# Transposing q and k of two pairs of heads by DMA, and placing the last batch's loads one by one, in a fused attention and mixing kernel

## The chip, the cores and the metric

One NeuronCore of a Trainium2 chip runs the kernel. The metric is the device time of one execution in microseconds (us). A time is 1.7 to 2.5 us longer than the span that the profile shows, which runs from the first to the last instruction. "At 88" means 88 us from the start of the span.

## The reference

Four batches, eight heads, 768 positions of 64 values. Causal attention within a window of 128 positions, with the first four positions always visible ("sinks"); its output is `x`, which a mixing layer takes:

```python
keep = is_sink | in_window
a = softmax(where(keep, q @ k.T / sqrt(64), -1e9))
x = a @ v                                   # heads side by side: 768 x 512 per batch
theta = x @ w_theta
zr, zi = x * cos(theta), x * sin(theta)
y = w_tok_r @ zr + w_tok_i @ zi             # along the sequence
u = x + y
out = u + maximum(u @ w_ch, 0)
```

## The kernel before

Heads go two by two, so there are 16 pairs: 8 to 11 are the third batch, 12 to 15 the last. A "slot" is the work on one pair, with a piece of the batch before's mixing woven in. The order on TensorE, ScalarE, GpSimd and SyncE is that of the program text; VectorE's order is made by a scheduler when the kernel is built. GpSimd casts q, k and v to bf16 ahead of their use. Tiles that the profile names: `sc` the scores, `E` their exponentials (ScalarE), `tp` a transpose of q or k by TensorE, `avp` the product with v, `x_nat` is x, `cs` cos and sin of theta (ScalarE; this part at the end of a batch's attention is the "phase stage"), `zz` holds zr and zi, `yp` sums y, `u` and `uT` are u and its transpose, `of` is the output.

q and k are needed with the 64 values of a head on the partitions, for two heads at once. TensorE transposes them into PSUM and ScalarE copies them out in another order of the columns; only the last batch's are transposed by DMA, straight into their final place, which asks for loads in rows of 256 bytes:

```python
QK_DMA = range(12, NPAIR)                   # pairs transposed by DMA, loaded in 256 byte rows
...
def transposed_by_dma(i):
    if i not in QK_DMA:
        return
    for name in ("q", "k"):
        c = qk_c.pop((name, i))             # bf16, cast by GpSimd
        x = qkt.tile([P, S], BF16, name=f"{name}T", tag=f"{name}T")
        nc.sync.dma_start_transpose(out=x.rearrange("c (t p) -> c t p", t=NT),
                                    in_=c.rearrange("p t h d -> p (t h d)"))
        qk_t[name, i] = x

def transposed(name, i):
    if i in QK_DMA:
        return
    c = qk_c.pop((name, i))
    tp = ps_sm.tile([P, NT, P], BF16, name="tp", tag="sm")
    for t in range(NT):
        nc.tensor.transpose(out=tp[:, t, :], in_=c[:, t, :, :], identity=ident)
    x = qkt.tile([P, S], BF16, name=f"{name}T", tag=f"{name}T")
    dst, src = x.rearrange("c (p t) -> c p t", t=NT), tp.rearrange("c t p -> c p t")
    ...
    nc.scalar.copy(out=dst, in_=src)        # VectorE for three early pairs
```

On the same SyncE queue are all loads but eight small ones of sink values, all stores of `of`, and two other transposes: `uT` (ahead of the product with `w_ch`, tile `wp`) and `xT` (ahead of `theta`, tile `thp`).

The values of the sinks of the third and last batch are put in place by VectorE, four instructions a batch, at the start of the third batch:

```python
def sink_values(b):
    for tb in range(NB):
        nc.vector.tensor_scalar(out=vsinks[b % 2][:, tb, :, 0:D], in0=vsf[:, b - 2, :, :],
                                scalar1=rows[:, tb:tb + 1], scalar2=None, op0=ALU.mult)
...
            if b > 1:
                slot(i, (p, hp))
                if b == 2 and hp < 2:
                    sink_values(2 + hp)
            else:
                ...
                if hp == 1:
                    load_later_sinks()      # loads vsf
...
        if b < 3:                           # at the end of the batch's attention
            for n in range(2):
                load_qk(HP * 3 + 2 * (b - 1) + n)
                load_v(HP * 3 + 2 * (b - 1) + n)
        thetas(b, 0)
```

The softmax here doesn't subtract the row's maximum and nothing guards it: scores larger than these inputs give would overflow.

## Time and profile before

| | before |
|---|---|
| median of 4 executions (range), us | 187.97 (187.84 to 188.6) |
| span in the profile, us | 186.9 |
| TensorE busy | 171.9 us, 92% |
| copy of q or k from PSUM on ScalarE, median | 0.80 us |

The part of the profile that counts here is the list of TensorE's waits: what it waited for, us in total, times, and the longest. The second line shown is the passage into the third batch, the first in part (0.6 of its 1.4 us) the passage into the last.

```profile
PE yp L350 <- DVE zz L321: 1.4, 3, 0.6
...
PE wp L378 <- DVE uT L371: 0.9, 1, 0.9
```

### The profile page before, as it was taken

Reading aid. Unit: us, or ns where it says so; the run is one execution under the profiler, and the core shown is the slowest. Engines: PE = TensorE matmul, PEld = TensorE weight load, DVE = VectorE, ACT = ScalarE, POOL = GpSimd, SP = SyncE. Lnnn points to the kernel's source line nnn. Section 1 sums busy time; section 2 is a strip of 40 time slices with the busy share of each in tenths; the row PEclk is TensorE's granted clock in tenths of the full one; section 3 lists DMA queues with packets and bytes.
Section 4 is the critical chain, followed back from the end, with each engine's and each line's share of the span. In section 5 each row is a group of like instructions: output and inputs, shape, how many; then the busy total and the mean of one; then the engine's idle time right before and its main releaser. Section 6 shows DMA issues by size and latency. Waiting matters only on the chain.

```text
span 186.9 us, 4095 instructions
## 1 busy us (share of the span) xinstructions
PE 171.9 (92%) x1655; PEld 88.8 (48%) x1655; DVE 125.7 (67%) x235; ACT 101.5 (54%) x109; POOL 68.7 (37%) x87
## 2 busy tenths in 40 slices
PE   6597998999998998997999999989999999999991
PEld 2344573544464655443455555423445554444550
DVE  6486776782967788189978683797786834824451
ACT  4876778617973661899855801797545019300000
POOL 8965468967886601314545001660000000000000
PEclk9999999999999999999999999999999999999997
DMA  5999999999999995990229769994654311034413
GB/s 183 310 299 205 308 394 345 369 354 334 355 360 340 283 245 154 282 207 4 68 65 165 168 100 271 282 194 59 150 119 100 98 60 56 0 87 109 141 59 114
DMA packets 68275, 36.42 MB, mean 195 GB/s; under 512 B 56352, under 2 KB 62752, under 8 KB 68256
## 3 DMA queue, kind: packets, MB, share of 16 engines
q1 hardware_dynamic: 66960, 35.99, 70.2%
q0 software_dynamic: 1152, 0.04, 0.5%
q8 instruction: 13, 0.21, 0.5%
q10 hardware_dynamic: 144, 0.13, 0.2%
q14 instruction: 6, 0.05, 0.1%
HBM read 25.82 MB, written 6.29 MB: 172 GB/s over the span
## 4 chain that ended last, share of the span: by engine, by line
PE 58%; DVE 14%; ACT 14%; DMA 6%; issue 3%; SPq 2%; POOL 0%; DVEq 0%; ACTq 0%
PE yp L350 22%; PE wp L378 9%; PE thp L308 8%; DMA vf<-in_v_dram 6%; PE avp L255 5%; PE sc L209 5%; DVE zz L321 4%; ACT E L222 4%; ACT cs L317 3%; ACT cs L318 3%; SPq L116 2%; PE tp L183 2%; DVE E L225 2%; PE xtp L285 2%; DVE vsink L467 2%
## 5 line engine op out<-in xcount | busy, mean ns | idle before, releaser
L222 ACT ACTIVATE E<-sc 128x1024 bf16<-128x1024 f32 x48 | 48.4, 1027 | 23.4 <-PE sc L209 17.5
L350 PE MATMUL yp<-zz,wrT 128*128 128x512 bf16 x138 | 52.4, 379 | 1.6 <-DVE zz L321 1.4
L350 PE MATMUL yp<-zz,wiT 128*128 128x512 bf16 x138 | 52.5, 380 | 0.4 <-ACT wiT L337 0.3
L225 DVE TENSOR_TENSOR E<-E,mask 128x768 bf16<-128x768 bf16 (+1 forms) x27 | 26.2, 981 | 13.2 <-ACT E L222 13.1
L75 POOL TENSOR_SCALAR q<-qf 128x768 bf16<-128x768 f32 x14 | 13.4, 958 | 44.2 <-PE tp L183 23.3
L321 DVE TENSOR_TENSOR zz<-cs,x_nat 128x1024 bf16<-128x1024 bf16 x24 | 20.2, 878 | 10.3 <-ACT cs L318 10.3
L378 PE MATMUL wp<-wch,uT 128*128 128x512 bf16 x92 | 23.6, 379 | 1.0 <-DVE uT L371 0.9
L381 DVE SCALAR_TENSOR_TENSOR of<-wp,u 128x512 f32<-128x512 f32 x23 | 15.8, 686 | 11.9 <-PE wp L378 11.7
L308 PE MATMUL thp<-wth,xT 128*128 128x512 bf16 x96 | 22.7, 379 | 0.4 <-ACT cs L318 0.4
L350 PEld LDWEIGHTS <-wiT 128*128 128x128 bf16 x138 | 13.5, 97 | 15.6 <-issue 3.3
L317 ACT ACTIVATE cs<-thp,half_pi 128x1024 bf16<-128x1024 f32 (+1 forms) x13 | 13.7, 1051 | 13.1 <-PE thp L308 12.8
L354 DVE TENSOR_TENSOR u<-yp,x_nat 128x512 bf16<-128x512 f32 x23 | 15.8, 687 | 6.7 <-PE yp L350 6.3
L75 POOL TENSOR_SCALAR vx<-vf 128x768 bf16<-128x768 f32 x16 | 18.8, 1174 | 2.2 <-DMA vf<-in_v_dram 2.2
L255 PEld LDWEIGHTS <-E 128*128 128x128 bf16 x480 | 17.1, 97 | 4.6 <-issue 1.6
L350 PEld LDWEIGHTS <-wrT 128*128 128x128 bf16 x138 | 13.5, 98 | 11.7 <-issue 1.5
L209 PE MATMUL sc<-qT,kT 64*128 64x256 bf16 x192 | 18.0, 265 | 1.0 <-ACT kT L187 0.8
L75 POOL TENSOR_SCALAR k<-kf 128x768 bf16<-128x768 f32 x14 | 12.7, 908 | 5.9 <-DMA kf<-in_k_dram 2.5
L308 PEld LDWEIGHTS <-xT 128*128 128x128 bf16 x96 | 9.1, 97 | 11.2 <-issue 0.9
L261 DVE TENSOR_TENSOR x_nat<-avp,rec 128x384 bf16<-128x384 f32 x27 | 14.2, 554 | 0.3
L209 PEld LDWEIGHTS <-kT 64*128 64x128 bf16 x192 | 5.6, 94 | 18.2 <-issue 14.4
L255 PE MATMUL avp<-vx,E 128*128 128x65 bf16 x297 | 13.2, 193 | 0.7 <-POOL vx L75 0.7
L318 ACT ACTIVATE cs<-thp 128x1024 bf16<-128x1024 f32 (+1 forms) x13 | 12.5, 958 | 0.0
(80 smaller groups left out, 192.8 us busy)
## 6 DMA issues: line engine op xcount, KB each, us to landing
qf<-in_q_dram SPq DMA_DIRECT2D x16, 384.0 KB, 5.4
kf<-in_k_dram SPq DMA_DIRECT2D x16, 384.0 KB, 6.1
vf<-in_v_dram SPq DMA_DIRECT2D x16, 384.0 KB, 6.8
out_dram<-of SPq DMA_DIRECT2D x23, 256.0 KB, 2.3
wf<-in_moe_w_tok_r_dram SPq DMA_DIRECT2D x6, 384.0 KB, 5.9
wf<-in_moe_w_tok_i_dram SPq DMA_DIRECT2D x6, 384.0 KB, 7.2
sqf<-in_moe_w_theta_dram SPq DMA_DIRECT2D x2, 512.0 KB
sqf<-in_moe_w_ch_dram SPq DMA_DIRECT2D x2, 512.0 KB, 6.4
```

The source lines that it names most:

```text
L75: nc.gpsimd.tensor_scalar(out=out, in0=in_, scalar1=1.0, scalar2=1.0, op0=ALU.mult, op1=ALU.mult)
L209: nc.tensor.matmul(sc[:, e, 256 * part:256 * part + n], lhsT=kT[r, m * P:(m + 1) * P], rhs=qT[r, m * P:m * P + n], start=not biased, stop= ...
L222: nc.scalar.activation(out=E[:, :, 512 * c:512 * (c + 1)], in_=sc, func=AF.Exp, scale=SCALE)
L225: nc.vector.tensor_tensor(out=E[:, :, r], in0=E[:, :, r], in1=mask2[:, :, r], op=ALU.mult)
L255: nc.tensor.matmul(avp[:, t, :], lhsT=lhsT, rhs=rhs, start=(j == 0), stop=(j == len(seq) - 1), skip_group_check=True)
L308: nc.tensor.matmul(th_t[b, g][:, st, :], lhsT=xT[:, cb, 2 * g + st, :], rhs=wth[:, cb, :], start=(cb == 0), stop=(cb == NC - 1))
L317: nc.scalar.activation(out=cs[:, part, 0, :], in_=thp[:, part, :], func=AF.Sin, bias=half_pi)
L318: nc.scalar.activation(out=cs[:, part, 1, :], in_=thp[:, part, :], func=AF.Sin)
L321: nc.vector.tensor_tensor(out=z_t[b][:, 2 * g + st, :, :].rearrange("p o (c n) -> p o c n", c=HP), in0=cs[:, st, :, :].rearrange("p o (c n ...
L350: nc.tensor.matmul(yp, lhsT=wT[i][:, t, sc, :], rhs=z_t[b][:, sc, i, :], start=(j == 0), stop=(j == 2 * NT - 1))
L354: nc.vector.tensor_tensor(out=u.rearrange("p (c n) -> p c n", c=HP), in0=yp.rearrange("p (c n) -> p c n", c=HP), in1=x_t[b][:, :, t, :], o ...
L378: nc.tensor.matmul(wp, lhsT=uT[:, cb, :], rhs=wch[:, cb, :], start=(cb == 0), stop=(cb == NC - 1))
```

## The change

The intent is to take work from TensorE, which is busy 92% of the time. The diff is cut to its core. q and k of pairs 10 and 11 go through a DMA transpose into a buffer `qr` or `kr` in SBUF ("raw": not yet in the wanted order of columns), and ScalarE's copy, which was there anyway, reorders them. Pairs 14 and 15 go the same way so that they can be loaded in rows of 1,536 bytes. To make room, one buffer for v goes, and the loads of pair 13 are moved from the end of the second batch into the third.

```diff
-    vstage = pool("vstage", 5)
+    vstage = pool("vstage", 4)
+    qkr = pool("qkr", 1)
-    QK_DMA = range(12, NPAIR)
+    QK_DMA = (12, 13)
+    QK_RAW = (10, 11, 14, 15)
     def transposed_by_dma(i):
+        if i in QK_RAW:
+            for name in ("q", "k"):
+                raw = qkr.tile([P, NT, P], BF16, name=f"{name}r", tag=f"{name}r")
+                nc.sync.dma_start_transpose(out=raw, in_=qk_c.pop((name, i)).rearrange("p t h d -> p (t h d)"))
+                qk_r[name, i] = raw
     def transposed(name, i):
+        if i in QK_RAW:
+            tp = qk_r.pop((name, i))
+        else:                               # the TensorE transposes, as before
                 slot(i, (p, hp))
                 if b == 2 and hp < 2:
                     sink_values(2 + hp)
+                if b == 2 and hp == 1:
+                    load_qk(HP * 3 + 1)
+                if b == 2 and hp == 2:
+                    load_v(HP * 3 + 1)
         if b < 3:
-            for n in range(2):
-                load_qk(HP * 3 + 2 * (b - 1) + n)
-                load_v(HP * 3 + 2 * (b - 1) + n)
+            for i in (HP * 3,) if b == 1 else (NPAIR - 2, NPAIR - 1):
+                load_pair(i)                # load_qk(i) and load_v(i)
```

More of the change, by code (lines that the diff above doesn't have):

```diff
@@ L102 @@
     qk_f, qk_c, qk_t, v_f, v_x, e_t = {}, {}, {}, {}, {}, {}
-    w_raw, x_t, xT_t, z_t, y_t, u_t, uT_t, th_t = {}, {}, {}, {}, {}, {}, {}, {}
+    w_raw, x_t, xT_t, z_t, y_t, u_t, uT_t, th_t, qk_r = {}, {}, {}, {}, {}, {}, {}, {}, {}
     def load_qk(i):
@@ L179, in transposed @@
             return
-        c = qk_c.pop((name, i))
-        tp = ps_sm.tile([P, NT, P], BF16, name="tp", tag="sm")
-        for t in range(NT):
-            nc.tensor.transpose(out=tp[:, t, :], in_=c[:, t, :, :], identity=ident)
+        if i in QK_RAW:
+            tp = qk_r.pop((name, i))
+        else:
+            c = qk_c.pop((name, i))
+            tp = ps_sm.tile([P, NT, P], BF16, name="tp", tag="sm")
+            for t in range(NT):
+                nc.tensor.transpose(out=tp[:, t, :], in_=c[:, t, :, :], identity=ident)
         x = qkt.tile([P, S], BF16, name=f"{name}T", tag=f"{name}T")
@@ L573, in slot, with load_pair @@
             pending.append(wtok)
+    def load_pair(i):
+        load_qk(i)
+        load_v(i)
     def warm(n):
```

## The prediction

"The lock" in it is the name for what the trace of before shows and no more: the two sink-value instructions beside GpSimd's casts took 1.06 us each, those with GpSimd idle 0.48, and the pair of `zz` at 123.18 took 2.44 beside two casts where the pair at 81.52 took 1.29. What holds VectorE up there is not shown.

> **What bounds the kernel now.** I read the page first, then the chain of waits, then the timelines of single engines in the stretches that the change touches. Times are us from the span's start. A "slot" is the work on one pair of heads; pairs 8 to 11 are the third batch, 12 to 15 the last.
>
> ```profile
> PE 171.9 (92%) x1655; PEld 88.8 (48%) x1655; DVE 125.7 (67%) x235; ACT 101.5 (54%) x109; POOL 68.7 (37%) x87
> PE   6597998999998998997999999989999999999991
> ```
>
> TensorE is busy for 92% of the span and bounds the kernel, except in slices below 9. Two of those matter here: the one around 87 (into the third batch) and the one around 124 (into the last). The chain of waits there:
>
> ```profile
> 85.01 2.72 DVE vsink L467 x4
> 87.73 0.34 DVE uT L371
> ...
> 88.12 1.04 PE wp L378 x4
> ...
> 90.24 0.34 PE tp L183 x6
> ...
> 91.65 0.34 PE tp L183 x6
> ...
> 96.70 0.34 PE tp L183 x6
> ...
> 98.12 0.34 PE tp L183 x6
> ...
> 123.18 1.23 DVE zz L321
> ...
> 124.45 0.38 PE yp L350
> ```
>
> The reader is to see two things. From 88.12 to 121 the chain is TensorE without a gap, and the four transpose groups in it (q and k of pairs 10 and 11) are exactly those that the change removes. And at both passages the chain runs through VectorE: TensorE waits for `uT` at 88.12 and for `zz` at 124.45. What VectorE does there, and GpSimd beside it, stands in their timelines:
>
> ```profile
> 84.70 1.01 POOL L75 TENSOR_SCALAR k<-kf 128x768 bf16<-128x768 f32 x1 [1.19 <-issue]
> 85.67 1.00 POOL L75 TENSOR_SCALAR vx<-vf 128x768 bf16<-128x768 f32 x1
> 90.72 1.42 POOL L75 TENSOR_SCALAR q<-qf 128x768 bf16<-128x768 f32 x1 [4.05 <-PE tp L183]
> ...
> 84.93 2.02 DVE L467 TENSOR_SCALAR vsink<-vsf,rows 128x512 bf16<-128x512 f32 x2
> ...
> 123.03 2.06 POOL L75 TENSOR_SCALAR vx<-vf 128x768 bf16<-128x768 f32 x2
> ...
> 123.18 2.44 DVE L321 TENSOR_TENSOR zz<-cs,x_nat 128x1024 bf16<-128x1024 bf16 x2 [0.21 <-ACT cs L318]
> ```
>
> Of the eight sink-value instructions the median is 0.476 us, but the two that overlap GpSimd's casts (84.70 to 86.67) take 1.06 each: 0.58 more per cast. The last two before `uT` have GpSimd idle and take 0.48. The pair of `zz` at 123.18 takes 2.44 beside two casts; the pair at 81.52 took 1.29 with GpSimd idle. GpSimd is idle from 86.67 to 90.72 only because the cast of pair 12 needs a cast buffer that TensorE's transposes of pair 10 free.
>
> [...] no copy of this shape from SBUF with a step between elements is in the trace of before. [...] 279 to 289 GB/s from 114 to 118, where rows are 256 bytes, and 324 GB/s from 57 to 60, with q and k in 1,536 byte rows.
>
> **The change part by part.**
>
> 1. Removed: 24 TensorE transposes. The four groups above take 0.34 us each on the path: 4 x 0.34 = 1.36 us less. The chain agrees: the whole slot with two groups runs from 95.63 to 102.09, 6.46 us; the one without, from 102.09 to 107.89, 5.80.
>
> 2. ScalarE. The four copies of pairs 10 and 11 stay, with their source in SBUF; four are added for pairs 14 and 15. One takes 0.80 from PSUM[...]. A slot then has 3 exponentials of 1.03 and 2 copies[...] against a slot of 5.8: not the bound. Cost on the path: 0.
>
> 3. The transposes by DMA. For pair 10 the casts are done by 77 and the queue has nothing to wait for after the loads of pair 12, so they land about 80 to 82, and ScalarE needs them after 90. For pair 11 the first copy out of the single raw buffer (about 92) and an output store must come first. Issues then take 1.26 us each and landing 2.6 to 3.6, so 97 and 98; ScalarE wants them at about 97.5 and 99. Tight, but I expect no wait that reaches TensorE.
>
> 4. The loads of pair 13 move from 76-80 to about 99-105, with q and k (1.4 us each, worked out from the spacing of landings in part 6) ahead of the transposes of pair 12 and of one `uT`. That `uT` would land about 106.4, needed at 106.8: 0 to 0.3 us, say 0.1.
>
> 5. What the diff does not name. The cast buffer of pair 10 is now freed by the DMA transposes (landed by 82) and not by TensorE at 90.6. So GpSimd runs the three casts of pair 12 and the next v right after 86.67, in place of 90.72. Two of them fall between the last two sink-value instructions before `uT`. By the pattern at 84.93 each costs 0.58: `uT` comes 2 x 0.58 = 1.16 us later. TensorE already waits there (0.90 us by the wait list), so all of it is on the path. Cost: 1.16 us.
>
> 6. The last batch's loads. GpSimd's casts at 116.08, 117.43, 120.40 and 121.82 start as their loads land: one load per 1.35 to 1.44 us, DMA being full from 112 to 124. At 320 GB/s the four long-row loads of 393 KB take about 1.2 us in place of 1.4 (an estimate from the rates above), so the last casts move about 0.8 us earlier against `zz`. The first `zz` at 123.18 took 1.23 in the chain and 0.68 in the clear: 0.55 lost to the lock, and about 0.15 more behind the second. Of these 0.7 I expect 0.45 back. More is not to be had: the first exponential of the last batch ends at 125.5 and holds the third scores, which now start at 126.2.
>
> 7. Not on the path: one v buffer fewer (each reused buffer was cast over 5 us before its next load), and VectorE's order in the third batch, where one mask product moves behind the normalisation. That batch leaves VectorE about 4.9 us of work per slot of 5.8.
>
> Sum: -1.36 + 0.1 + 1.16 - 0.45 = -0.55 us, 187.92 becoming 187.4.
>
> **The rivals.** A, the plain reading: TensorE is the bound, 24 transposes go, nothing else reaches the path: with part 6, -1.8 us, 186.1. For it: the gapless chain after 88. Against it: the copied pattern of the lock at 84.93. B, the lock bites, as summed: 187.4. C, the queue becomes the wait: in-order issue on SyncE with 1.26 us per transpose makes the copies of pair 11 or a `uT` late, ScalarE stalls before an exponential, and TensorE with it; 0.5 to 1.5 us more than B, 188 to 189. For it: the margins of 0.4 us in parts 3 and 4. D, ScalarE reads SBUF with a 256 byte step slowly, say twice 0.80: then 3.09 + 3.2 = 6.3 us per slot, ScalarE bounds four slots and costs about 0.5 us each, 2 us over B, 189.4. Against it: from PSUM the same step costs nothing, 0.80 against 0.796 for a contiguous copy of that size (`xT`).
>
> **Range and chances.** I give B about 60%, A 25% and C and D together 15%. The mean lies a little below B: 187.2. The range from A to a mild C is 186.0 to 188.3. Two per cent is 3.8 us; no sum of parts 1 and 6 comes near it, and slower by that much needs D at its worst. Chances: faster 0.02, same 0.95, slower 0.03.
>
> **What would show it.** In the changed profile: no `tp` group of pairs 10 and 11, and slots of 5.8 us in the chain from about 90 on (1); [...] GpSimd's q cast starting at about 86.7 instead of 90.72 and sink-value instructions of about 1.06 just before `uT`, with `wp` starting near 89.3 (5); a shorter `zz` pair after 123 (6). If `wp` still starts at 88.1, part 5 is wrong and A holds; if TensorE's idle time names ScalarE's copy or a DMA between 95 and 107, C holds.

## The result, and the profile after

The changed kernel took 192.56 us (median of four, 192.37 to 192.79) where the kernel before took 187.97 beside it: a ratio of 1.0238, with a 95% interval of 1.0212 to 1.0264. It is slower by 2.4%, and 4.3 us above the upper end of the predicted range. Ratios here are the mean time of one kernel's fast executions over that of the other's in the same rounds, so they are not quite the ratio of the medians. Executions over 1.5% slower than the fastest of the same kernel are left out of the means.

Where the time went is found by taking the same instructions in both traces as milestones: the first exponential of a pair, a fixed sine of the third batch's phase stage, the last copy `lT` (near the end of the kernel). The table gives the time from one to the next, in us; the last column is the best version, which comes later. Each column is one profiled execution: that of before was the longest of its four (188.6), that of e11 the shortest of its four (186.04), so the spans of these two differ by more than the kernels do. The first stretch varies from 83.6 to 86.8 in the sixteen traces, by 0.7 between two traces of one kernel (e11 and e15).

| stretch | before | after | e11 |
|---|---|---|---|
| start to first exponential of pair 8 | 85.6 | 85.4 | 85.1 |
| to that of pair 9 | 3.9 | 5.0 | 3.4 |
| to that of pair 11 | 12.9 | 11.6 | 11.3 |
| to the sine in the third batch's phases | 13.7 | 17.2 | 13.7 |
| to first exponential of pair 13 | 12.0 | 11.6 | 11.5 |
| to the last `lT` | 54.2 | 54.2 | 54.2 |
| to the end of the span | 4.6 | 5.7 | 5.0 |
| span | 186.9 | 190.7 | 184.2 |

The gain that was wanted is there: 1.3 us in the stretch that loses the transposes. Two stretches give back more: 1.1 us before pair 9 and 3.5 before the sine. A third loss, 1.1, is at the very end. TensorE's wait list after, to be held against the one of before:

```profile
PE wp L389 <- DMA uT<-u: 2.7, 1, 2.7
PE wp L389 <- DVE uT L382: 2.0, 1, 2.0
...
PE thp L319 <- DMA xT<-x_nat: 0.8, 1, 0.8
```

Three waits, and they are the two stretches: the wait for VectorE's `uT` grew from 0.9 to 2.0, and two waits for DMA, 2.7 and 0.8, are new. The busy time of TensorE from 105 to 119 says the same. In these rows of the table by stretch the columns are the stretch, its length, and the busy us of TensorE matmuls, weight loads, VectorE, ScalarE and GpSimd with the count of instructions, then clock, DMA share and GB/s. First before, then after:

```profile
105.00:119.00 14.00, 14.00 (x138) 7.79 (x135) 9.27 (x20) 4.64 (x5) 2.40 (x3) 1.00 0.93 202
```

```profile
105.00:119.00 14.00, 10.49 (x110) 6.12 (x110) 7.46 (x17) 2.24 (x2) 2.90 (x3) 1.00 1.03 185
```

14.00 of 14.00 us busy became 10.49, so 3.5 us idle, at an undiminished clock. The chain of waits of the changed kernel goes through the three places:

```profile
84.74 3.86 DVE vsink L478 x4
88.60 0.33 DVE uT L382
...
88.98 1.04 PE wp L389 x4
...
106.49 2.43 DMA uT<-u
...
114.19 3.45 DMA xT<-x_nat
```

Before, four sink-value instructions took 2.72 us at this point, now 3.86. GpSimd and VectorE side by side show why, in the timeline of the changed kernel:

```profile
86.36 1.00 POOL L76 TENSOR_SCALAR q<-qf 128x768 bf16<-128x768 f32 x1
87.32 0.99 POOL L76 TENSOR_SCALAR k<-kf 128x768 bf16<-128x768 f32 x1
...
84.66 3.94 DVE L478 TENSOR_SCALAR vsink<-vsf,rows 128x512 bf16<-128x512 f32 x4
```

GpSimd's casts of pair 12 come at 86.36 instead of 90.72, and all four sink-value instructions, about 0.98 us each, run beside casts; with GpSimd idle, in the kernel before, one took 0.48. The two waits for DMA are read from SyncE's queue, with the VectorE instruction that makes `u` ahead of it:

```profile
100.73 0.68 DVE L365 TENSOR_TENSOR u<-yp,x_nat 128x512 bf16<-128x512 f32 x1
```

```profile
99.81 0.43 SPq L114 DMA_DIRECT2D qf<-in_q_dram  x1
100.28 0.85 SPq L114 DMA_DIRECT2D kf<-in_k_dram  x1
101.24 3.82 SPq L181 DMA_TRANSPOSE qT<-q  x1
105.16 1.24 SPq L181 DMA_TRANSPOSE kT<-k  x1
106.49 1.22 SPq L371 DMA_TRANSPOSE uT<-u  x1
```

`u` is complete at 101.41, but its transpose is issued at 106.49: two loads and the transposes of pair 12 stand ahead of it, and the issue of the one behind the loads took 3.82 us. In the kernel before, `u` of this slot is complete at 101.10, and the same instructions stand so:

```profile
98.46 1.70 SPq L173 DMA_TRANSPOSE qT<-q  x1
...
101.58 1.23 SPq L360 DMA_TRANSPOSE uT<-u  x1
```

Nine us later the same happens in the changed kernel with the load of pair 13's v, a transpose issue of 2.53, and `xT`. An issue is not always 1.25 us where no load is ahead, either: in the kernel before, that of `xT` at 108.49 took 2.32 and that of `qT` at 98.46 took 1.70, and in two later runs `qT` took 2.15 (e11) and 2.70 (e13).

Last, ScalarE's copies from `qr` and `kr`, with smallest, median and largest duration in ns:

```profile
L198 ACT COPY qT<-qr x4: 1500/1530/1545, 91.3 to 137.5; 128x768 bf16<-128x768 bf16 x4
```

They take 1.53 us, where the copy from PSUM took 0.80. It is not SBUF alone: in the kernel before, ScalarE's one cast of `q` (128x768, fp32 to bf16), read from SBUF in rows without a step, took 0.83.

### The profile page after: what moved, and what is told of

Read it like the earlier page. It is cut to its first block, busy times and chain, and to the rows that moved or that the text cites. A ratio compares the mean times of both kernels' runs of the same rounds, so it can differ in the third digit from the quotient of the medians.

```text
span 190.7 us, 4027 instructions
## 1 busy us (share of the span) xinstructions
PE 169.6 (89%) x1604; PEld 87.6 (46%) x1631; DVE 125.5 (66%) x235; ACT 109.5 (57%) x113; POOL 68.4 (36%) x87
## 4 chain that ended last, share of the span: by engine, by line
PE 53%; DVE 15%; ACT 14%; DMA 8%; issue 4%; SPq 2%; POOL 1%; DVEq 0%; ACTq 0%
PE yp L361 22%; PE wp L389 9%; PE thp L319 6%; DMA vf<-in_v_dram 5%; PE sc L220 5%; PE avp L266 4%; DVE zz L332 4%; ACT E L233 4%; ACT cs L328 3%; ACT cs L329 3%; DVE vsink L478 2%; DVE u L365 2%; SPq L119 2%; DVE E L236 2%; PE tp L194 2%
## 5 line engine op out<-in xcount | busy, mean ns | idle before, releaser
L361 PE MATMUL yp<-zz,wrT 128*128 128x512 bf16 x134 | 50.8, 379 | 1.0 <-DVE zz L332 0.5
L361 PE MATMUL yp<-zz,wiT 128*128 128x512 bf16 x131 | 49.8, 380 | 0.9 <-DVE wiT L350 0.4
L236 DVE TENSOR_TENSOR E<-E,mask 128x768 bf16<-128x768 bf16 (+1 forms) x27 | 24.6, 922 | 12.0 <-ACT E L233 12.0
L76 POOL TENSOR_SCALAR q<-qf 128x768 bf16<-128x768 f32 x14 | 13.7, 976 | 50.2 <-DMA qf<-in_q_dram 32.7
L389 PE MATMUL wp<-wch,uT 128*128 128x512 bf16 x81 | 21.9, 379 | 5.3 <-DMA uT<-u 2.7
L328 ACT ACTIVATE cs<-thp,half_pi 128x1024 bf16<-128x1024 f32 (+1 forms) x13 | 13.7, 1050 | 16.2 <-PE thp L319 15.6
L76 POOL TENSOR_SCALAR vx<-vf 128x768 bf16<-128x768 f32 x16 | 17.9, 1119 | 1.7 <-DMA vf<-in_v_dram 1.7
L76 POOL TENSOR_SCALAR k<-kf 128x768 bf16<-128x768 f32 x14 | 13.4, 954 | 5.1 <-DMA kf<-in_k_dram 1.5
L389 PEld LDWEIGHTS <-uT 128*128 128x128 bf16 x92 | 7.8, 97 | 12.5 <-DVE uT L382 3.2
```

The costliest lines, as they stand in the source:

```text
L76: nc.gpsimd.tensor_scalar(out=out, in0=in_, scalar1=1.0, scalar2=1.0, op0=ALU.mult, op1=ALU.mult)
L236: nc.vector.tensor_tensor(out=E[:, :, r], in0=E[:, :, r], in1=mask2[:, :, r], op=ALU.mult)
L328: nc.scalar.activation(out=cs[:, part, 0, :], in_=thp[:, part, :], func=AF.Sin, bias=half_pi)
L361: nc.tensor.matmul(yp, lhsT=wT[i][:, t, sc, :], rhs=z_t[b][:, sc, i, :], start=(j == 0), stop=(j == 2 * NT - 1))
L389: nc.tensor.matmul(wp, lhsT=uT[:, cb, :], rhs=wch[:, cb, :], start=(cb == 0), stop=(cb == NC - 1))
```

## The experiments

Two repairs are at the centre of what follows. One undoes the late loads of pair 13 or puts them on another queue; the other moves the sink-value instructions away from GpSimd's casts. "Theory Q" is the order on the SyncE queue, "theory L" that VectorE's sink-value instructions take longer beside GpSimd's casts (0.98 us against 0.48). In the texts of what was expected, "E9" is the first exponential of pair 9, and "reads" are the sink-value instructions.

### e1: pair 13 loaded early again

```diff
-                if b == 2 and hp == 1:
-                    load_qk(HP * 3 + 1)
-                if b == 2 and hp == 2:
-                    load_v(HP * 3 + 1)
...
-            for i in (HP * 3,) if b == 1 else (NPAIR - 2, NPAIR - 1):
+            for i in (HP * 3, HP * 3 + 1) if b == 1 else (NPAIR - 2, NPAIR - 1):
```

> The changed kernel with one part undone: q, k and v of pair 13 are loaded with those of pair 12 at the end of the second batch, as before. Theory Q (the SyncE queue is first in, first out: the loads of pair 13 stand ahead of the transposes of pairs 12 and 13 and so ahead of one uT and one xT): the 2.65 us wait of wp for uT and the 0.8 us wait of thp for xT go, so about 3.4 us less than the changed kernel, 189.1; the issue of qT of pair 12 takes about 1.3 us and not 3.82. Rival S (ScalarE, whose copies from SBUF take 1.53 us, is the bound): the late loads do not matter, 192 to 192.5.

Measured: 189.78 (188.5 to 190.09), ratio to before 1.0085 (1.003 to 1.0141). Both waits for DMA are gone from the wait list, the issue of pair 12's `qT` took 1.26 us, and the stretch from pair 11 to the sine is 13.7 us instead of 17.2. This supports theory Q. The median fell by 2.8 us, where 3.4 were expected. What is left over the kernel before is the wait for VectorE's `uT`, 2.0 us as in the changed kernel, and something new: from 87.78 to 91.19 the granted clock was 0.5.

### e2: only the late loads, on the kernel before

The kernel before with the changed placing of pair 13's loads, `QK_RAW = ()` and `QK_DMA = range(12, NPAIR)`.

> The kernel before with nothing changed but the place of the loads of pair 13 (and one v buffer fewer): no raw transposes, no copies from SBUF. Theory Q: the same two waits appear, 2.5 to 4 us slower than before, 190.5 to 192. Rival S: no change, 188.

Measured: 189.18 (187.93 to 189.58), ratio 1.0075 (1.0022 to 1.0127). It lost less than expected, and not where expected: no wait for `uT` or `xT` by DMA. In its trace 1.2 us are lost in the slot of pair 10 (7.66 against 6.47), in another wait:

```profile
100.47 0.30 PE L266 MATMUL avp<-vsink,E 128*128 128x65 bf16 x4 [1.02 <-DVE x_nat L272]
```

TensorE's order in this kernel is that of the kernel before, instruction by instruction, but VectorE's scheduler placed a mask product and the normalisations (`x_nat`) otherwise, and the PSUM buffer that `x_nat` reads came free late. Without the raw transposes ahead of them the two loads were issued at 97.04 instead of 99.81, and the issue behind them took 2.05 us; `uT` landed in time. By e1 and e2 together the waits for DMA in the changed kernel need both: late loads and the four extra transposes on the same queue. As e2 also has VectorE's other order, this does not rest on one difference alone.

### e3: raw transposes for the last batch only

e1 with `QK_RAW = (14, 15)`.

> Loads of pair 13 early; raw DMA transposes with ScalarE copies and long rows for pairs 14 and 15 alone; pairs 10 and 11 on TensorE as before. Part 6 of the prediction: the zz wait after 123 shrinks, 0.3 to 0.6 us faster than before, 187.5. Rival S: four copies of 1.53 us make two slots of the last batch longer by 0.3 us or more each, 188.6.

Measured: 187.77 (187.02 to 188.78), ratio 0.9995 (0.994 to 1.005): the same. In its trace the passage to pair 13 is shorter by 0.3 us, which the noise of the executions hides. Nor would it show the long rows at work: kernels that load the last batch in rows of 256 bytes, as before, have 11.42 us (e12) to 12.09 (e10) there, those with long rows for pairs 14 and 15 have 11.46 (e1, e7, e11) to 12.12 (e13, e15).

### e4: raw transposes for the third batch only

e1 with `QK_RAW = (10, 11)` and `QK_DMA = range(12, NPAIR)`.

> Raw DMA transposes for pairs 10 and 11 alone; the last batch loaded and transposed as before. Lock theory (part 5): 24 transposes less, 1.36 us less, and the GpSimd casts of pair 12 among the sink-value instructions, 1.16 us more: 187.8, wp after the passage starting about 1.1 us later than in the kernel before. If the lock costs nothing: 186.6. Rival S: over 189.

Measured: 190.99 (190.11 to 191.81), ratio 1.0162 (1.0106 to 1.0218), 3.2 us over what was expected. The stretched sink values are there (3.94 us for four), and behind them is what the expectation did not have. In the timeline of TensorE:

```profile
90.40 1.20 PE L389 MATMUL wp<-wch,uT 128*128 128x512 bf16 x4 [2.04 <-DVE uT L382]
91.53 0.61 PE L220 MATMUL sc<-qT,kT 64*128 64x256 bf16 x4
92.07 0.61 PE L361 MATMUL yp<-zz,wrT 128*128 128x512 bf16 x1
```

The product `yp` takes 0.38 us elsewhere and 0.61 here. The granted clock is 0.5 from 91.14 to 94.55. Over all the traces there are six such half-rate episodes ahead of the end, in e1, e4 (two), e5, e7 and e8, all 3.41 us long at 0.5, and in the 3.41 us ahead of each TensorE was busy for 0.30 to 0.58 of the time. For five of the six a wait for `uT` of 1.8 to 2.0 us lies wholly or for the most part in that stretch; e4's first, from 9.22, is in the start of the kernel. From pair 8 to pair 10 it took 12.3 us here and 12.1 in e1, against 10.8 in the changed kernel, which has the same wait of 2.0 us and no episode; so an episode costs about 1.3 to 1.5. It is not the cause of the changed kernel's time: its profiled execution, 192.44, has none ahead of the end, even after its wait of 2.65 us. In the 3.41 us from 105.51 to 108.92, where `uT` landed, TensorE was busy for 1.03 us, a share of 0.30, and in those from 106.20 for 0.76, 0.22, and the granted clock stayed at 1.00; so the busy share of the 3.41 us ahead does not by itself tell whether half rate follows. What sets it off stays open.

### e5 and e6: the sink values on GpSimd

e5 is e4, and e6 the kernel before, with

```diff
-            nc.vector.tensor_scalar(out=vsinks[b % 2][:, tb, :, 0:D], in0=vsf[:, b - 2, :, :],
+            nc.gpsimd.tensor_scalar(out=vsinks[b % 2][:, tb, :, 0:D], in0=vsf[:, b - 2, :, :],
...
-                if b == 2 and hp < 2:
-                    sink_values(2 + hp)
...
+        if b == 1:
+            sink_values(3)
+            sink_values(2)
         if b < 3:                           # ahead of the loads at the end of the second batch
```

> e4 (only the third batch's two pairs go by DMA; last batch as before; all loads early) with the two sink-value reads of the third batch moved from VectorE to GpSimd and to the end of the second batch. Theory L (GpSimd casts of the third batch now fall into the sink-value reads of VectorE, which stretch from 2.72 to 3.9 us for four and delay uT): the reads are gone from VectorE, E9 comes 1.3 to 1.8 us earlier than in e4, the median falls from 190.99 to about 188.0 or below, and against the kernel before with the same move (the next run) it is lower by 0.8 to 1.4 us, which is the TensorE transposes' worth. Rival theory D (the slow ScalarE copies of 1.5 us or the DMA transposes themselves cost): it stays above the next run by 1 us or more. A half-clock episode of 3.41 us can add about 1 us to either; it is looked up in the clock row.

> The kernel before with only the sink-value reads of the third batch moved from VectorE to GpSimd and to the end of the second batch. It takes away the 0.9 us in which TensorE waits for uT near 87 us in the kernel before. Theory L: about 186.9 (186.6 to 187.4). Rival: the wait moves to another engine and the time stays at 187.9 (GpSimd work beside VectorE slows VectorE's masks at the end of the second batch).

Measured: e5 192.71 (191.74 to 192.95), ratio 1.0221 (1.0168 to 1.0273); e6 187.58 (187.35 to 188.17), ratio 0.9963 (0.9914 to 1.0011). e6 lies between its theory (186.9) and its rival (187.9), and by its interval it is not apart from the kernel before. By the letter of the expectation e5 speaks for theory D. Its timeline says that the experiment itself was badly chosen. On GpSimd a sink-value instruction takes 1.56 us (median), the eight of them 13.7, so the casts behind them come late, the load of a v buffer that a cast frees comes late, and the raw transposes of pair 10 come at 89.80, ahead of a `uT` whose `u` was complete at 87.90:

```profile
89.80 2.17 SPq L174 DMA_TRANSPOSE qr<-q  x1
...
93.40 1.21 SPq L371 DMA_TRANSPOSE uT<-u  x1
...
95.88 1.67 PE L389 MATMUL wp<-wch,uT 128*128 128x512 bf16 x4 [1.90 <-DMA uT<-u]
```

The wait for VectorE's `uT` is gone, as theory L says, and a wait for a DMA's `uT` of 1.90 us took its place one slot later, followed by a half-rate episode. So e5 shows nothing against L; it shows Q once more, with transposes instead of loads ahead of `uT`. e10 to e12 repeat the question without this fault.

### e7: the late loads on ScalarE's queue

The changed kernel, with the loads of pair 13 issued by ScalarE:

```diff
-                    load_qk(HP * 3 + 1)
+                    load_qk(HP * 3 + 1, nc.scalar)
-                    load_v(HP * 3 + 1)
+                    load_v(HP * 3 + 1, nc.scalar)
```

> The changed kernel with only the queue of pair 13's three late loads changed from the SyncE queue to the ScalarE queue. Theory Q (the transposes uT and xT are late because the SyncE queue works in order[...]): the issue of qT12 falls from 3.82 to about 1.3 us, the uT wait of 2.65 us near 109 falls below 0.8, and the median falls from 192.56 to 190.2 (189.6 to 191.0). Rival theory T (the transposes are slow because any load in flight holds them, whichever queue it came from; or GpSimd's late cast of q makes them late): the issue stays at 3 us or more and the median within 0.5 of 192.56.

Measured: 190.02 (188.39 to 190.97), ratio 1.0104 (1.0044 to 1.0165): 2.5 us less than the changed kernel, close to the 190.2 that theory Q named. SyncE's queue:

```profile
98.53 1.27 SPq L183 DMA_TRANSPOSE qT<-q  x1
99.89 1.24 SPq L183 DMA_TRANSPOSE kT<-k  x1
101.38 1.73 SPq L373 DMA_TRANSPOSE uT<-u  x1
```

`u` of this slot is complete at 101.35, and its transpose is issued at 101.38, not 5.1 us later. No wait for a DMA is left on TensorE. Besides the queue one more thing changed: ScalarE reaches the loads at 93.42, so they are also 6.4 us earlier than in the changed kernel (v's 9.4). The run shows that the loads, where they stood on SyncE's queue, are the cause; it does not separate their order from their hour. The other queue is not free: the slot of pair 10 is 6.4 us long here and 6.2 in e13 below, against 5.8 in the changed kernel and 5.7 in e11, and in both ScalarE waited for a raw transpose (0.67 and 0.41 us).

### e8: all of the change, with loads early and sink values on GpSimd

e1 with the edit of e5.

> Both raw parts (third and last batch), pair 13 loaded early as before, and the sink-value reads on GpSimd at the end of the second batch: the change without the two things that the trace blames. If these two are the whole loss, the -1.36 us of the transposes and the -0.3 us of the long rows show: 186.9 of the run before it minus 1.7, so about 185.4 (184.8 to 186.3), faster than e6. If the slow ScalarE copies or the DMA transposes cost by themselves, it is at e6's time or above.

Measured: 190.62 (188.51 to 193.94), ratio 1.0082 (0.9999 to 1.0165). The median of the three fast executions is 190.10. Missed by about 5 us, for the reason found in e5: a wait of 1.8 us for a DMA's `uT`, then half rate from 96.11 to 99.52. It is also the run with the widest spread, and the longer executions have the lower clock: 188.51, 190.10, 191.14 and 193.94 us at a mean granted clock of 0.997, 0.991, 0.984 and 0.968 (the last counts as slow). The timed executions have no trace, so where their half-rate stretches lay is not shown.

### e10 to e13: the sink values earlier, on VectorE

The phase stage at the end of the second batch leaves VectorE idle for 4.0 us. The eight instructions go there, and their load goes one pair earlier:

```diff
-                if b == 2 and hp < 2:
-                    sink_values(2 + hp)
...
-                if hp == 1:
+                if hp == 0:
                     load_later_sinks()
...
+        if b == 1:
+            sink_values(2)
+            sink_values(3)
         if b < 3:
```

e10 is the kernel before with this edit, e11 is e1, e12 is e4, e13 is e7.

> The kernel before with the sink-value reads of the third and fourth batch kept on VectorE but moved to the phase stage at the end of the second batch, where VectorE is idle for 4 us (their load goes one pair earlier). GpSimd is untouched. If the reads near 85 us are what delays u and uT, TensorE's 0.9 us wait for uT near 87 us goes: 187.0 (186.7 to 187.5). Risk: eight reads of about 0.5 us do not quite fit in the 4 us and push zz of the third batch by 0.5 us: then 187.5 to 188.

> Both raw parts, pair 13 loaded early as before, the same move of the sink-value reads on VectorE. GpSimd keeps its order, so unlike in the run with the reads on GpSimd the loads and casts of the third batch are not delayed. Theory (lock on the reads, order of the queue, and half-rate after long waits are the whole loss): E9 0.8 us earlier than in the kernel before, no half-rate episode near 88 to 97 us, median 1.4 to 1.7 below e10: 185.4 (184.9 to 186.2). Rival (DMA transposes of raw q and k and the slow ScalarE copies make their own waits for uT and kT): a wait for uT or kT of over 1 us stays between 85 and 100 us and the median is 187.5 or above.

> Only the third batch's raw pairs, last batch as before, sink-value reads moved on VectorE: theory 0.3 above e11, 185.8 (185.3 to 186.5); rival as for e11, 187.5 or above. Against e4 (190.99), which differs only in the reads, theory says -4 to -5 us, of which about 1.2 is the stretched reads and the rest half-rate episodes and the wait.

> The changed kernel with the two repairs together: pair 13's late loads on the ScalarE queue and the sink-value reads moved on VectorE. Both causes of the trace are gone, so it should be within 0.5 us of e11: 185.7 (185.0 to 186.7). If the late placing has a cost apart from the order of the SyncE queue, it lies above e11 by more than 0.7.

| run | median (range), us | ratio to before (95%) | the same kernel without the edit, median |
|---|---|---|---|
| e10 | 187.69 (186.81 to 188.37) | 0.9970 (0.9920 to 1.0021) | 188.19, the kernel before in the same rounds |
| e11 | 186.91 (186.04 to 187.95) | 0.9950 (0.9897 to 1.0003) | 189.78, e1 |
| e12 | 187.32 (186.40 to 187.88) | 0.9949 (0.9899 to 0.9998) | 190.99, e4 |
| e13 | 187.35 (185.84 to 188.15) | 0.9946 (0.9885 to 1.0006) | 190.02, e7 |

The edit is worth 2.7 to 3.7 us with raw pairs in the third batch and little in the kernel before. In e11's timeline of VectorE the sink values now lie in the idle stretch, and `uT` comes as soon as TensorE has made it:

```profile
75.23 3.05 DVE L478 TENSOR_SCALAR vsink<-vsf,rows 128x512 bf16<-128x512 f32 x5
...
85.42 0.42 DVE L382 COPY uT<-utp 128x512 bf16<-128x512 bf16 x1 [0.94 <-PE utp L380]
```

In none of the four traces is a wait for `uT` among the seven largest, and none has a half-rate episode ahead of the end. So the edit takes away three things together: the stretch, the wait, and the episode that the wait can bring. By the milestones, pair 9 to pair 11 takes 11.3 us in e11; in e10's trace it is 12.6. The difference is 1.3, which is the value of 24 TensorE transposes. ScalarE's copies of 1.53 us are still in e11 and cost nothing there.

All four missed their expectations by 0.7 to 1.7 us on the high side. e10, which has none of the change, falls into the range that was named as its risk; its trace, 0.6 us shorter than that of the kernel before, does not show a cause. e11 and e12 lie between theory and rival, whose limit of 187.5 they do not reach, and the waits that the rival asked for are not there. e12 is 3.7 us under e4, where 4 to 5 were expected. e13 is within 0.5 of e11, as expected. Part of their miss is the end of the kernel. From the last `lT` to the end of the span, the five traces without raw pairs in the third batch (before, e2, e3, e6, e10) have 4.57 to 4.62 us and the eleven with them 4.85 to 5.73 (5.02 and 5.69 in two traces of one kernel, e11 and e15). Among the packets of the last store lies one of the DMA queue that the page calls "q14 instruction", both in the changed kernel (0.66 us long) and in the kernel before (0.47), so what causes it stays open.

### e14 and e15: the missing cell, and the best version again

e14 is the changed kernel with the edit of e10 alone. e15 is e11 with more rounds.

> The changed kernel with only the sink-value reads moved early on VectorE; pair 13's late loads stay on the SyncE queue. With the changed kernel (192.56), e7 (other queue, 190.02) and e13 (both, 187.35) this fills a table of two by two. If the two causes add up: 192.56 minus 2.7 (what the move gave from e7 to e13) is 189.9 (189.2 to 190.6), with the waits for uT near 109 us and for xT near 117 us still there. If the late loads were only harmful because the stretched reads came first, it falls to 188 or below.

> The same kernel as e11 with more rounds, for the final comparison with the kernel before: 186.9 (186.5 to 187.3), ratio 0.994 (0.990 to 0.997). Repeats are the question, not a mechanism: whether the gain is over the noise of the executions.

Measured: e14 189.70 (189.31 to 190.52), ratio 1.0091 (1.0059 to 1.0122). e15 187.01 (186.04 to 188.44), ratio 0.9929 (0.9892 to 0.9965). e14 keeps the DMA waits:

```profile
PE wp L389 <- DMA uT<-u: 2.1, 1, 2.1
...
PE thp L319 <- DMA xT<-x_nat: 0.9, 1, 0.9
```

Medians in us, two by two:

| | sink values at the start of the third batch | in the phase stage |
|---|---|---|
| pair 13's late loads on SyncE | 192.56 (the changed kernel) | 189.70 (e14) |
| on ScalarE's queue | 190.02 (e7) | 187.35 (e13) |

Each repair gives about the same with and without the other: 2.9 and 2.7 for the sink values, 2.5 and 2.4 for the loads. Alone they sum to 5.4, together they gave 5.2. The four were timed in different rounds, on at least three chips; as ratios to the kernel before beside them they are 1.0238, 1.0091, 1.0104 and 0.9946, which says the same. The two causes add up, and together they outweigh the 4.6 us lost. Not all of what the sink-value edit gives is loss undone, though: in the kernel before it takes 0.8 us from the stretch from pair 8 to pair 10 (e10's trace), a wait that was there already. The best version is e11, which loads pair 13 early: in e15 0.7% faster than the kernel before, apart from 1 by its interval.

## Why the prediction was wrong

It said 187.2 and got 192.56. By its own parts:

1. Right. The stretch without the transposes is 1.3 us shorter (1.36 predicted), with slots of 5.8 us in it.
2. Wrong in size, right in consequence, and that by luck. A copy from SBUF took 1.53 us, against 0.80 from PSUM and close to rival D's "twice 0.80"; that it would be no bound was the estimate. By the part's own sum a slot would then be 3.09 + 2 x 1.53 = 6.2 us, over 5.8. But neither this nor D's sum was borne out: instructions on ScalarE start before the one ahead has ended (exponentials of 1.03 us start 0.92 apart), ScalarE was busy for 13.6 of the 15 us from 90 to 105, and the slots stayed at 5.8. The trace of before had no copy from SBUF with a step between elements, only the cast of 0.83 without one.
3. Right as written: the raw transposes landed in time for ScalarE. It asked whether they are late, not what waits behind them.
4. This is the step that failed: "That `uT` would land about 106.4, needed at 106.8: 0 to 0.3 us, say 0.1". It landed at 108.92 and TensorE waited 2.65 us. The `xT` behind the late v was not considered at all, and TensorE waited another 0.80. The working took each transpose as an issue of 1.26 us. Behind a load the issue took 3.82 and 2.53. The first alone is 2.56 more than assumed, which is by how much `uT` landed late; the trace of before already had issues of 1.70 and 2.32. Part 4 measured 3.5 us, not 0.1. Rival C named the mechanism, in-order issue on SyncE, but sized it at 0.5 to 1.5 us, and gave C and D together 15%.
5. Right, including the 1.16: the wait for `uT` grew from 0.9 to 2.0 us. Moving the sink values away gave more than this, 2.7 to 3.7 us by the medians: it also takes the wait that the kernel before had, and in e1, e4 and e7 the half-rate episode. In the changed kernel, whose trace has no episode, it gave 2.9, of which the two profiled executions (192.44 and e14's 190.52, the longest of its six) show 1.8 between pair 8 and pair 10; the rest is not explained.
6. Open. The passage into the last batch gained 0.3 us in the changed kernel and 0.5 in e1 and e11, predicted 0.45; but in e15's trace, of the same kernel as e11, it gained nothing (12.1 us against 12.0), and kernels without the long rows gained as much: 0.5 in e2, e5 and e12. So no gain is shown. The sign that was named, a shorter `zz` pair after 123, is there in the changed kernel (1.93 us for 2.44) and equally in e2 (1.93), which has rows of 256 bytes.
7. VectorE's new order was named as harmless. In the changed kernel it was, but e2 lost 1.2 us to another such order.

Not in the prediction: the longer end of the kernel, 1.1 us in the profile.

The sum by what was measured in the trace: -1.3 (1) + 3.5 (4) + 1.1 (5) - 0.3 (the stretch of 6) - 0.3 (start) + 1.1 (end) = 3.8 us; the spans differ by 190.7 - 186.9 = 3.8. The medians differ by 4.6, because the profiled execution of before was the longest of its four.

## What to carry to other kernels

A transpose or load that is moved onto a queue like SyncE's here, whose issues follow one another, has two costs, its own landing and the delay of everything behind it (`uT` was issued 5.1 us after `u` was complete): list what stands behind it, and for each the time at which its data is ready. A buffer that is freed earlier sets another engine going earlier (GpSimd's cast came at 86.36 instead of 90.72); ask what that engine will then run beside. And a wait of two us on TensorE can cost more than it lasts: in five of these traces the granted clock was 0.5 for 3.41 us after one of 1.8 to 2.0.
